# Decoding float64 weights with two rectifiers and an AND in place of three activations, with four of the five hand-written orders dealt anew

## The chip, the cores and the metric

The kernel runs on one core of a Trainium2 chip. Its engines are TensorE (PE, with its weight loads shown apart as PEld), VectorE (DVE), ScalarE (ACT), GpSimd (POOL) and SyncE (SP, which here only issues DMAs). The metric is device time in microseconds (us), the median of several runs. Before the change it is 758.82 us, the median of 3 runs from 758.43 to 759.01.

## The reference

Attention between tokens and a small recurrent state, in both directions, followed by a gated feed-forward layer:

```python
B, H, S, Ns, D = (8, 8, 512, 32, 64)
scores = scale * np.matmul(x, state.transpose(0, 1, 3, 2))
a = softmax(scores);  xread = np.matmul(a, state)
scores2 = scale * np.matmul(state, x.transpose(0, 1, 3, 2))
a2 = softmax(scores2); sread = np.matmul(a2, x)
x = concatenate([xread, sread])      # as (B*S', H*D) rows, S' = 512 + 32
rms = np.sqrt(np.mean(x * x, axis=-1, keepdims=True) + 1e-06)
xn = x / rms * rms_g
silu = g * (1.0 / (1.0 + np.exp(-g)))          # g = xn @ w_gate
return (silu * (xn @ w_val) @ w_out).astype(np.float32)
```

There are 4352 rows of 512, and 1536 hidden columns. The three weight matrices arrive as float64 values, two 32-bit words to each number, while the rest is float32. [...]

## The kernel before, in words

**Weights.** The three matrices are read as 18 pieces of 1 MB ("raw", four buffers; piece 0 in two halves). Each piece holds 128x1024 numbers. `exponents()` (lines 231 to 248) works on ScalarE: it takes the top 16 bits of each number (sign, eleven bits of exponent, four of mantissa) and, in three activations, L240, L243 and L246, turns them into the 16 bits of a bfloat16 that is a signed power of two. Prelu is a rectifier with another slope on its negative side, and `FLAT` sets the ratio of the two slopes. `values()` (lines 250 to 282) works on VectorE: L267 masks the top mantissa bits and puts the leading one in, L270 adds the low word to 2^32 times that, and L276 multiplies the mantissa by the power of two from ScalarE and writes the float32 weight. Every third piece ends with a write of the finished weights to DRAM (L280), from which later batches fetch them (`fetch`, L189). Conversion tiles (`conv`) have two buffers each.

**Batches.** Eight batches of 512 tokens follow each other. For batch b the kernel computes the reading of the state (`tokens_read`: scores L361, maximum, EXP, sums, transposes, the squares of what is read, their sum, a power on POOL at L293, its turning back along rows on PE at L300, and the scaling at L501). For batches after the first the sum of the squares goes through `rms_on_blocks`: a block sum on PE (L415), `ss` on VectorE (L420), `mean_root` on POOL (L293), `along_rows` on PE (L300). `states_read` is the other direction; L557 and L572 are its products. Because the state has 32 rows and the weights are reused, the weights are first multiplied by the batch's state (`own_weights`, products L616, copies L628 on ScalarE, sums L643 to L646 on POOL), and tokens then multiply by these.

Batch 0 runs plain: `hidden` (products L659 for gate and value, silu L665, gated product L669 on VectorE, PSUM pool `vps` of two banks) and `project_as_ready` (L866). Later batches use schemes with seven products: `hidden_seven` (products L763, copies L810, L813 and L815 out of PSUM on ScalarE, silu L817, sums L826 and L839 on VectorE) and `project_twice` (products L1066, copies L1076 into tiles "kept", combination L1092 to L1097 on POOL, and `stores()` by L1174). The hidden layer of a batch runs in six groups. The tiles "g" of `hidden_seven` and the tiles "kept" of blocks p1, u2 and c21 share the two buffers of tag "g". The block c21 is the last of a batch, so its buffer is the one that group 1 of the next batch writes next (L810).

**Order.** Each engine runs its instructions in the order in which they are issued, SyncE too, and the kernel issues them in an order written out by hand. Every stretch of work is a Python generator, called by a letter, and a string of letters says which generator takes its next step. In ORDER (batch 0 and all conversion) "e" is one step of `exponents`, "d" one of `values`, "z" a filler product on PE (`keep_awake`, L1198), "a" and "s" the readings for batch 0, "A" and "S" those for batch 1, "v" `own_weights`, "h", "t", "u" products, silu and gated product of the hidden layer, "p" and "c" projection, "w" the first steps of batch 1 and "k" sums of weights. FIRST is the string of batch 1, PERIOD that of batches 2 to 6, LAST that of batch 7, and STATES that of the state rows. In these "h", "t", "u" are products, copies and sums of `hidden_seven`, "p", "c", "k", "o" are products, copies, sums and stores of `project_twice`, "v" and "x" products and copies of `own_weights`, "w" the first products of the next batch, "a" and "s" the readings for the next batch, "f" a fetch of weights (L189), "g" a fetch of a weight quarter (L1012), and "l" the loads of state and x (L129, L134). Letters of different engines set no order between those engines; waits for data and for free buffers do that.

Of the kernel before, what the change touches and what calls it, by code (L numbers as in the profile page):

```python
# [8 lines left out]
F32 = mybir.dt.float32  # L9
I32 = mybir.dt.int32  # L10
U32 = mybir.dt.uint32
U16 = mybir.dt.uint16
I16 = mybir.dt.int16
BF16 = mybir.dt.bfloat16
ALU = mybir.AluOpType
ACTF = mybir.ActivationFunctionType
# [3 lines left out]
P = 128  # L20
RAW_AHEAD = 4
W_BUFS = 3
FLAT = 1793.0

ORDER = (
    "ddzzzzzzzzzezzzeezaaaaaaaaaaaaddaezddaseaaazzaeaaazzdaaaazdeezzzazzaaaazeeaaaadd"
    "aaadaaeAdadsdeezezAdavaaAvAAAAvhehteeAeAdddduhhppdAddtdeeedvvvudeeedphhdtheeddtA"
    "ddddeupdAAAdhAdedeeuedppvpsdAvvddAedhhpetudeeeddhtsAAdhudpAeppdddeAAeedddvAdsvvA"
    "eedphhtuseessseedddeeAhtsdhesppsdvdupdvvdhheeAddAdAtsshtpAudApAedpdhededdveuAApA"
    "AAvvheAdAtSAASSeSSdphSddShAtASuShAkuSSwwpwwkcpSScpSkkckpkcwkkkkkwwwwk"  # L30
)

PERIOD = (
    "vlhhatthhtaxxhvuxuthhthuhtauuhhtuhuhuthtahtuaaahuhhtuhuhuxhxtutxhthukkkhtaakavfx"
    "xxvgahuhuthuuuxhthhuuxtahtaaaaahuaxhuthhtuhhthhthhsppusuuuuffutaauuhpsspuppppukp"
    "ukkkkckkaakkgppkkcpppakooskakakakkppppacpppappppcckpfppcakakapppaakkkasskkgkaagg"
    "pppppppppppaakakkooakgapssskaaakkkoosspppcfpaawwsslpssxxxpcoowxxxfg"
)

FIRST = (  # L40
# [4 lines left out]
    "xssswxlscxxcoxofxg"  # L45
)
LAST = (
    "vxhhffththhtuhhhavuttuuhhtfuhhgxxthhhuuuxxtuthuhtthuhuxhutuvxxxvhthhutkxghhtuhut"
    "kxxhuukhtuhthhthhhhhuuuuttuthhhuuuuhtuhuutuupphuukkppcpapkkkkkpppppppppppkkkpcpp"
    "ckkppkckpkkpkpckkkpppkkkpkoppkpppagcpppppfkpkkkkkkkkppaaaapkpggppppacpcggooooooo"  # L50
    "a"
)
STATES = (
    "hththtyyhuhuhhttuhhhyyytyuhutuhhhutthtuyyhhuuyhhthhhuyututyyyhhtyuhhthuuuhhuhtth"
    "ythuuuyyyutuhuhuytuuyhthhuuhthtuhuhutuuppkhpuucppkkccpkpkpc"
)


# [1 line left out]
def kernel(  # L60
# [21 lines left out]
    VE, SE, GE, TE = nc.vector, nc.scalar, nc.gpsimd, nc.tensor  # L82
# [13 lines left out]
    consts = ctx.enter_context(tc.tile_pool(name="consts", bufs=1))  # L96
# [34 lines left out]
    def load_x(b, *queues):  # L131
# [6 lines left out]
        for c in range(NC):  # L138
# [10 lines left out]

    GE.tensor_tensor(out=consts.tile([P, NC], F32, name="first_pow"), in1=mhalf,  # L150
                     in0=ones.to_broadcast([P, NC]), op=ALU.pow)
    bounds = consts.tile([P, 3], F32, name="bounds")
    for i, bound in enumerate((-896.0 - 7.5 / 16, 1.0, 255.0 * 128)):
        GE.memset(bounds[:, i:i + 1], bound)
    rms_g = consts.tile([P, NI], F32, name="rms_g")

# [22 lines left out]
    raw = {}  # L179
# [11 lines left out]
    def home(k):  # L191

        mp, kind = divmod(k, 3)
        if kind == 2:
            return wo[:, 2 * mp:2 * mp + 2].rearrange("p m (i f) -> p m i f", f=P)
        return (w_sb[mp] if kind else new_w(mp))[:, :, :, kind, :]
# [12 lines left out]
    def load_piece(k):  # L209
        for _ in load_parts(k):  # L210
            pass

    def parts(k):

        n = pieces[k].shape[1]
        return (slice(0, n // 2), slice(n // 2, n)) if k == 0 else (slice(0, n),)
# [3 lines left out]
    exs = {}  # L220

    def columns(k, a):
        n = pieces[k].shape[1]
        return slice(8 * P * a.start // n, 8 * P * a.stop // n)

    def exponents():

        for k in range(len(pieces)):  # L230
            for a in parts(k):
                if k not in raw:
                    yield from range(3)
                    continue
                if a.start == 0:
                    exs[k] = conv.tile([P, 8 * P], I16, name="ex")
                    lin = conv.tile([P, 8 * P], F32, name="lin")
                ex, line = exs[k][:, columns(k, a)], lin[:, columns(k, a)]
                half = raw[k][:, columns(k, a)].bitcast(I16)[:, :, 3::4]
                SE.activation(out=line, in_=half, func=ACTF.Prelu, scale=1.0 / 16,  # L240
                              bias=bounds[:, 0:1], alpha=1.0 / FLAT)
                yield
                SE.activation(out=ex, in_=line, func=ACTF.Prelu, bias=bounds[:, 1:2],  # L243
                              alpha=FLAT)
                yield
                SE.activation(out=ex.bitcast(U16), in_=ex, func=ACTF.Relu, scale=128.0,  # L246
                              bias=bounds[:, 2:3])
                yield

    def values():  # L250
        for k in range(len(pieces)):
            for a in parts(k):
                if a.start == 0:
                    to = home(k)
                    if k in raw:
                        top_ = conv.tile([P, 8 * P], I32, name="top")
                dst = to[:, a]
                if k not in raw:
                    src = pieces[k].rearrange("p a (c f) -> p a c f", f=P)
                    for i in range(a.start, a.stop):  # L260
                        nc.sync.dma_start(out=to[:, i], in_=src[:, i])
                    yield from range(3)
                else:
                    top, r = (t[:, columns(k, a)] for t in (top_, raw[k]))
                    hi = r[:, :, 1]
                    man = r.bitcast(F32)[:, :, 0]
                    VE.tensor_scalar(top, hi, 0xfffff, 0x100000,  # L267
                                     op0=ALU.bitwise_and, op1=ALU.bitwise_or)
                    yield
                    VE.scalar_tensor_tensor(out=man, in0=top, scalar=2.0 ** 32,  # L270
                                            in1=r.bitcast(U32)[:, :, 0], op0=ALU.mult, op1=ALU.add)
                    yield
                    yield
                    man, ex = (t.rearrange("p (a c f) -> p a c f", f=P, c=dst.shape[2])
                               for t in (man, exs[k][:, columns(k, a)].bitcast(BF16)))
                    VE.scalar_tensor_tensor(out=dst, in0=man, scalar=-2.0 ** -52, in1=ex,  # L276
                                            op0=ALU.mult, op1=ALU.mult)
                if a.stop == pieces[k].shape[1]:
                    if k % 3 == 1:
                        nc.sync.dma_start(out=w_d[k // 3], in_=w_sb[k // 3])  # L280
                    raw.pop(k, None)
                    load_piece(k + RAW_AHEAD)
                yield
# [887 lines left out]
    def store_tokens(b):  # L1171
        def store(r, c0, n, ot):
            rows_ = out[T * b:T * b + S, c0:c0 + n]
            nc.sync.dma_start(out=rows_[P * r:P * r + P], in_=ot)  # L1174
        return store
# [48 lines left out]
    for k in range(2, RAW_AHEAD):  # L1224
        load_piece(k)
    load_state(1)
    load_x(1)
    streams = {"a": tokens_read(0), "s": states_read(0), "A": tokens_read(1), "S": states_read(1),
               "e": exponents(), "d": values(),
               "v": (step for mp in range(NM // 2) for part in own_weights(0, mp) for step in part),  # L1230
               "h": of_batch_0(0), "t": of_batch_0(1), "u": of_batch_0(2),
# [5 lines left out]
    with tc.manual_schedule(**by_hand):  # L1237
# [7 lines left out]
        for b in range(1, B):  # L1245
            h, t, u = hidden_seven(S, weights_of(b), lambda b=b: tokens_of(b), True)
            p, c, k, o = project_twice(b, store_tokens(b))
# [19 lines left out]
        p, c, k = project_seven(NT, store_states, nc.scalar)  # L1267
# [34 lines left out]
```

## Time and profile before

| | |
|---|---|
| time, median of 3 | 758.82 us |
| span of the profiled execution | 756.2 us |
| PE busy in 0 to 32.5 us | 27.64 us |
| PE busy in 32.5 to 133 us | 100.45 us |
| PE busy in 133 to 213 us (batch 1) | 76.44 us |
| PE busy in 293 to 373 us | 80.00 us |
| PE busy in 614 to 756 us | 138.31 us |
| granted TensorE clock, every window | 1.00 |

The profiled execution spans 756.2 us from the first to the last instruction; against the median some 2.6 us lie around it. Batch 1 starts at 133 us, and a batch in PERIOD takes about 80 us. In the lines of the profile the letter L with a number is the line of the kernel; a group has its count after x, then the busy time in us, the mean duration in ns, and the idle time of the engine ahead of it with what ended it. In the timeline the first number is the start in us, the second the duration. A "DMA issues" line ends with the median time from issue to landing.

### The profile page before, as it was taken

What the parts mean: (1) busy time and instruction counts of PE and PEld (TensorE: products, weight loads), DVE (VectorE), ACT (ScalarE), POOL (GpSimd) and SP (SyncE); (2) the same over time, 40 slices, a digit from 0 to 9 for tenths busy, and PEclk for the clock granted to TensorE, in tenths of its full rate; (3) what the DMA queues carried; (4) which work ended last, traced back from release to release, by engine and by line L of the source; (5) the groups of instructions that cost most, each with busy time, mean ns of one, the idle gap of its engine ahead of it and who ended that gap; (6) DMA issues with size and microseconds to landing.
All of it is one profiled execution on the core that took longest, in us unless ns stands there. A gap on an engine that the chain in (4) does not pass through costs nothing.

```text
span 756.2 us, 14360 instructions
## 1 busy us (share of the span) xinstructions
PE 743.2 (98%) x5618; PEld 592.0 (78%) x5618; DVE 578.7 (77%) x979; ACT 351.7 (47%) x546; POOL 294.2 (39%) x380
## 2 busy tenths in 40 slices
PE   8999999999899999999999999999999999999998
PEld 6534444778768898879877997799788987899997
DVE  3887776679957996689947994799579965787961
ACT  5998965553235523643255425543456236411220
POOL 2000003892584326532474129312842275323600
PEclk9999999999999999999999999999999999999999
DMA  9986954695576176725684377517661865132311
GB/s 281 281 299 227 314 211 151 248 294 163 201 228 240 32 291 209 281 56 198 243 284 112 135 274 253 175 69 299 215 225 27 305 204 218 51 98 114 140 56 29
DMA packets 61891, 146.17 MB, mean 193 GB/s; under 512 B 15744, under 2 KB 32640, under 8 KB 54912
## 3 DMA queue, kind: packets, MB, share of 16 engines
q1 hardware_dynamic: 48704, 125.78, 47.8%
q10 hardware_dynamic: 13120, 19.47, 8.9%
q8 instruction: 45, 0.74, 0.4%
q14 instruction: 22, 0.18, 0.1%
HBM read 116.46 MB, written 28.77 MB: 192 GB/s over the span
## 4 chain that ended last, share of the span: by engine, by line
PE 91%; DVE 5%; ACT 3%; issue 1%; POOL 0%; DVEq 0%; POOLq 0%
PE f L763 38%; PE f L1066 28%; PE pv L659 5%; PE f L866 5%; PE at L616 3%; PE pv L616 3%; PE f L929 2%; PE f L1198 2%; PE at L557 1%; PE at L361 1%; PE at L487 1%; DVE hb L1125 0%; PE at L300 0%; ACT ex L243 0%; PE at L334 0%
## 5 line engine op out<-in xcount | busy, mean ns | idle before, releaser
L763 PE MATMUL f<-aT_s,v 128*128 128x256 f32 x504 | 119.6, 382 | 0.0
L763 PEld LDWEIGHTS f<-aT_s,v 128*128 128x128 f32 x504 | 94.5, 190 | 24.8 <-issue 8.4
L1092 POOL TENSOR_TENSOR kept<-kept 128x256 f32<-128x256 f32 x28 | 23.1, 824 | 174.9 <-DVE kept L1106 173.8
L826 DVE TENSOR_TENSOR g<-g,f 128x512 f32<-128x512 f32 x84 | 57.4, 686 | 40.0 <-PE f L763 35.9
L1076 ACT COPY kept<-f 128x512 f32<-128x512 f32 (+1 forms) x56 | 29.6, 532 | 123.9 <-PE f L1066 82.2
L763 PE MATMUL f<-aT_t,vs 128*128 128x256 f32 x336 | 87.1, 383 | 0.0
L1066 PE MATMUL f<-w,h 128*128 128x128 f32 x588 | 74.6, 276 | 0.9 <-DVE h L1116 0.8
L763 PEld LDWEIGHTS f<-aT_t,vs 128*128 128x128 f32 x336 | 62.5, 190 | 15.4 <-POOL vs L643 4.2
L1066 PEld LDWEIGHTS f<-w,h 128*128 128x128 f32 x588 | 69.6, 192 | 5.3 <-issue 4.1
L817 ACT ACTIVATE hb<-g 128x1024 f32<-128x1024 f32 x42 | 44.4, 1058 | 56.9 <-DVE g L826 56.8
L643 POOL TENSOR_TENSOR vs<-v 128x256 f32<-128x256 f32 x42 | 31.4, 748 | 79.5 <-ACT v L628 79.5
L293 POOL TENSOR_TENSOR ri<-ss,mhalf 128x4 f32<-128x4 f32 x8 | 10.7, 1341 | 116.7 <-DMA w_m<-w_d 84.1
L815 ACT COPY g<-f 128x512 f32<-128x512 f32 x42 | 24.6, 586 | 45.0 <-PE f L763 45.0
L763 PE MATMUL f<-aT_t,v 128*128 128x256 f32 x168 | 43.5, 381 | 1.6 <-DVE c L826 1.6
L866 PE MATMUL f<-wo,hb 128*128 128x512 f32 x96 | 44.8, 603 | 0.0
L659 PE MATMUL pv<-aT_s,v 128*128 128x512 f32 x96 | 43.9, 595 | 0.0
L763 PE MATMUL f<-aT_s,vs 128*128 128x256 f32 x168 | 43.6, 382 | 0.0
L839 DVE TENSOR_TENSOR hb<-hb,c 128x512 f32<-128x512 f32 (+1 forms) x48 | 36.6, 763 | 7.9 <-ACT hb L817 7.2
L839 DVE TENSOR_TENSOR hb<-hb,f 128x512 f32<-128x512 f32 (+1 forms) x48 | 31.0, 646 | 15.1 <-PE f L763 15.1
L1066 PE MATMUL f<-wo,h 128*128 128x128 f32 x336 | 42.2, 275 | 0.0
L1066 PE MATMUL f<-wo,hb 128*128 128x128 f32 x336 | 42.1, 275 | 0.0
L826 DVE TENSOR_TENSOR c<-c,f 128x512 f32<-128x512 f32 (+1 forms) x48 | 31.2, 651 | 12.6 <-PE f L763 12.6
(204 smaller groups left out, 1657.7 us busy)
## 6 DMA issues: line engine op xcount, KB each, us to landing
w_m<-w_d SPq DMA_DIRECT2D x48, 1024.0 KB, 5.8
w<-t_d SPq DMA_DIRECT2D x49, 576.0 KB, 5.1
out_dram<-kept SPq DMA_DIRECT2D x56, 128.0 KB, 1.9
raw<-in_moe_w_val_dram SPq DMA_DIRECT2D x6, 1024.0 KB, 5.4
raw<-in_moe_w_out_dram SPq DMA_DIRECT2D x6, 1024.0 KB, 8.5
w_d<-w_m SPq DMA_DIRECT2D x6, 1024.0 KB, 4.9
x_b<-in_x_dram SPq DMA_DIRECT2D x6, 1024.0 KB, 7.7
x_d<-xB ACTq DMA_DIRECT2D x6, 1024.0 KB, 4.2
```

Of the source, the lines that this page charges most:

```text
L616: TE.matmul(out=pv[e][Ns * j:Ns * j + Ns, :], lhsT=stT_g[b][D * e:D * e + D, j, :], rhs=w[D * e:D * e + D, j].rearrange("p m k f -> p (m k ...
L643: GE.tensor_tensor(out=vs[:, 0], in0=a21, in1=a22, op=ALU.add)
L659: TE.matmul(out=to[0], lhsT=lhs(i, k), rhs=r, start=(i == 0), stop=(i == len(rhs) - 1))
L763: TE.matmul(out=ps[:, i, 0:half], lhsT=l[:, i, :], rhs=r, start=(start and i == 0 and k == 0), stop=(k == len(lhs) - 1), skip_group_check= ...
L815: SE.copy(gates(q)[1], q["x"][:, :, 0:half])
L817: SE.activation(out=hb[:, 2 * mp:2 * mp + 2, 0:n].rearrange("p m (c t) -> p m c t", c=2), in_=q["g"][:, :, :, 0:half], func=ACTF.Silu if s ...
L826: VE.tensor_tensor(out=to, in0=to, in1=q[ps][:, :, 0:half], op=ALU.add)
L839: VE.tensor_tensor(out=part, in0=part, in1=val, op=ALU.mult)
L866: TE.matmul(out=banks[r], lhsT=hb[:, m, P * r:P * r + P], rhs=wo[:, m, :], start=(m == 0), stop=(m == NM - 1))
L1066: TE.matmul(out=to[half][:, slot, :], lhsT=lhs[:, k, :], rhs=rhs[:, k, :], start=(fresh and n in (0, 4) and k == 0), stop=(k == QM - 1), s ...
L1076: SE.copy(k[:, 4 * i:4 * i + 4 - i], banks[name][i])
L1092: GE.tensor_tensor(out=k[:, 1:3], in0=k[:, 0:1].to_broadcast([P, 2, QD]), in1=k[:, 1:3], op=ALU.add)
```

## The change

`exponents()` uses two activations instead of three. The first now reads the top 16 bits as unsigned and with a negative scale, the second brings the result straight into the 16 bits of a bfloat16, in a form that has bits too many; `values()` then clears these with one bitwise AND on VectorE, in place, on the two-byte numbers taken as 512 32-bit words in each partition (256 for the halves of piece 0), between L270's and L276's places. The constants follow (`FLAT`, and two columns of `bounds` instead of three). The letter "e" has two steps per piece in place of three: 38 in place of 57 in ORDER. ORDER, PERIOD, LAST and STATES are dealt anew; FIRST is not touched. PERIOD, LAST and STATES hold the same letters as before in another order.

```diff
-FLAT = 1793.0
+FLAT = 128.0 * 1792.0
...
 ORDER = (
-    "ddzzzzzzzzzezzzeezaaaaaaaaaaaaddaezddaseaaazzaeaaazzdaaaazdeezzzazzaaaazeeaaaadd"
-    "aaadaaeAdadsdeezezAdavaaAvAAAAvhehteeAeAdddduhhppdAddtdeeedvvvudeeedphhdtheeddtA"
-    "ddddeupdAAAdhAdedeeuedppvpsdAvvddAedhhpetudeeeddhtsAAdhudpAeppdddeAAeedddvAdsvvA"
-    "eedphhtuseessseedddeeAhtsdhesppsdvdupdvvdhheeAddAdAtsshtpAudApAedpdhededdveuAApA"
-    "AAvvheAdAtSAASSeSSdphSddShAtASuShAkuSSwwpwwkcpSScpSkkckpkcwkkkkkwwwwk"
+    "eezzzzdzdzzzzzdaazadaaaaaaaaazezdadeazadadaazaeaazzzaaazzezaazzzaazazaaazadaadee"
+    "aadaaAdaedasseAAAvvvaAAasAdAdhhAhtsddeudpdsdddedtAepdhudvvdevphdesephtddAshededd"
+    "uAhAApAddtddvSpdedusAvvhethdhphdeAddedteAddSesueASddupAppddedAdvevddveAdAphthdSd"
+    "AsseedSpudAsddApepvedhvSdtAvhAhuSdehApdAtAdepAehASAuddddedAtSdAhdpvpvAvdhhduAete"
+    "uSphAdtAhpAdkusAppccApSwkskwSSkwkpkSkwwcwkwkwckkkw"
 )
 
 PERIOD = (
-    "vlhhatthhtaxxhvuxuthhthuhtauuhhtuhuhuthtahtuaaahuhhtuhuhuxhxtutxhthukkkhtaakavfx"
-    "xxvgahuhuthuuuxhthhuuxtahtaaaaahuaxhuthhtuhhthhthhsppusuuuuffutaauuhpsspuppppukp"
-    "ukkkkckkaakkgppkkcpppakooskakakakkppppacpppappppcckpfppcakakapppaakkkasskkgkaagg"
-    "pppppppppppaakakkooakgapssskaaakkkoosspppcfpaawwsslpssxxxpcoowxxxfg"
+    "vaxhahththtfhuhuhhutaahtaxhttauhhuaxvuuhxhhttuhgtuhhxhxtuhuuhtauhhaututkkvvhtxah"
+    "xxuhuhhhautxhtahxkuuuktaahautashhuuuthstuxhhfguhtutuhahuutahuususpaphlpukfpakppk"
+    "pcpckppkpupaafkpkkkkppkkapgppcppakkkkkkppppappsacpappacakpakkgasppkapksppakpkpck"
+    "pooaapkpakapogaksappkapakakaagposkpkspssaawsosowsglppfwcxxsxcfxoxox"
 )
...
-    bounds = consts.tile([P, 3], F32, name="bounds")
-    for i, bound in enumerate((-896.0 - 7.5 / 16, 1.0, 255.0 * 128)):
+    bounds = consts.tile([P, 2], F32, name="bounds")
+    for i, bound in enumerate((1152.0 - 1.0 / 32, -FLAT)):
...
                 if k not in raw:
-                    yield from range(3)
+                    yield from range(2)
...
-                half = raw[k][:, columns(k, a)].bitcast(I16)[:, :, 3::4]
-                SE.activation(out=line, in_=half, func=ACTF.Prelu, scale=1.0 / 16,
+                half = raw[k][:, columns(k, a)].bitcast(U16)[:, :, 3::4]
+                SE.activation(out=line, in_=half, func=ACTF.Prelu, scale=-1.0 / 16,
                               bias=bounds[:, 0:1], alpha=1.0 / FLAT)
                 yield
-                SE.activation(out=ex, in_=line, func=ACTF.Prelu, bias=bounds[:, 1:2],
-                              alpha=FLAT)
-                yield
-                SE.activation(out=ex.bitcast(U16), in_=ex, func=ACTF.Relu, scale=128.0,
-                              bias=bounds[:, 2:3])
+                SE.activation(out=ex, in_=line, func=ACTF.Prelu, scale=-128.0 * FLAT,
+                              bias=bounds[:, 1:2], alpha=1.0 / FLAT)
                 yield
...
                     yield
+                    bits = exs[k][:, columns(k, a)].bitcast(I32)
+                    VE.tensor_scalar(bits, bits, -0x7f0080, None, op0=ALU.bitwise_and)
                     yield
```

LAST and STATES are left out of the diff: their letters are as many of each as before, in another order. The AND takes the step that was empty in `values()` before, so the letter "d" keeps its number of steps.

## The prediction

> **What bounds the kernel now.** I read the page from its head down: the busy shares, the chain that ended last, then the groups of the first stretch, and after them the timeline and the DMA issues around one boundary between two batches.
>
> ```profile
> PE 743.2 (98%) x5618; PEld 592.0 (78%) x5618; DVE 578.7 (77%) x979; ACT 351.7 (47%) x546; POOL 294.2 (39%) x380
> PE 91%; DVE 5%; ACT 3%; issue 1%; POOL 0%; DVEq 0%; POOLq 0%
> ```
>
> TensorE is busy for 98% of the span and carries 91% of the chain. A saving on ScalarE or VectorE is worth something only where TensorE waits, and a new order of the work is worth what it adds to or takes from those waits. A table of windows shows where they are: PE is busy 80.00 of 80 us from 293 to 373 and again from 373 to 453, 100.45 of 100.5 from 32.5 to 133, and only 27.64 of the first 32.5. So the first 32.5 us can give something; the batches of PERIOD can only lose.
>
> ```profile
> L240 ACT ACTIVATE lin<-raw,bounds 128x1024 f32<-128x1024 int16 x17 | 21.2, 1249 | 0.0
> L270 DVE SCALAR_TENSOR_TENSOR raw<-top,raw 128x1024 f32<-128x1024 int32 x17 | 20.9, 1226 | 0.3
> L243 ACT ACTIVATE ex<-lin,bounds 128x1024 int16<-128x1024 f32 x17 | 19.6, 1153 | 0.4
> L246 ACT ACTIVATE ex<-ex,bounds 128x1024 uint16<-128x1024 int16 x17 | 19.5, 1148 | 0.3
> L267 DVE TENSOR_SCALAR top<-raw 128x512 int32<-128x512 int32 x2 | 1.0, 522 | 5.1 <-DMA raw<-in_moe_w_gate_dram 5.1
> ```
>
> These are the groups of the conversion, forms kept apart. The third activation, L246, goes.
>
> **The sum is made against** the profiled execution: span 756.2 us plus 2.6 us around it, 758.8, which is the median.
>
> **Part 1, the conversion.** ScalarE loses 17 x 1.148 + 2 x 0.726 = 21.0 us. VectorE gains 19 ANDs, 17 of 128x512 int32. No row shows an AND alone; L267, two bit operations on the same shape, took 522 ns on average, and 687 at twice the width. I take 0.52 (bounds 0.43, the faster of the two, and 0.69), so about 9.4 us of VectorE. None of it counts as such: from 32.5 to 133 VectorE is busy 74.6 and ScalarE 81.4 of 100.5 us, and PE covers both. If that cover goes, an AND costs its 0.52 in each chain it stands in. The other constants cost nothing: same two operations, same shapes.
>
> **Part 2, the start (new ORDER).** PE's first 32.5 us are one chain: the state and x turned, scores, exponentials, squares, the root mean square, and the first hidden product, L659, at 32.46.
>
> ```profile
> 9.33 0.27 PE L311 MATMUL at<-ident,rows 128*128 128x128 f32 x1
> 28.50 1.40 POOL L293 TENSOR_TENSOR ri<-ss,mhalf 128x4 f32<-128x4 f32 x1 [22.67 <-DVE ss L397]
> 32.46 1.88 PE L659 MATMUL pv<-aT_s,v 128*128 128x512 f32 x4
> ```
>
> Before L311 stand 13 of the idle fillers (z, L1198). The new order has 10; the early ones take 427 ns a record, so L311 moves from 9.33 to about 8.05 (the state rows landed at 8.04), 1.3 us. Further on, the turned x waits for one activation less on ScalarE, and the conversion's last product L276 (1.22 us, at 27.03) no longer stands between the second square (26.43) and ss (28.26). Followed by hand through the new letters: scores 13.36 becomes 12.3, the maximum 15.87 becomes 15.0, ss 28.26 becomes 26.9, the pow 28.50 becomes 27.1, L659 about 30.4. A gain of 2.05 (1.5 to 2.5). The raw pieces are issued in the same order, so no new wait on DMA.
>
> Against it stands one new wait. Hidden group 5's value product needs the PSUM bank (two in the pool) that group 4's gated product, L669, must first read. On VectorE that L669 now stands behind the AND and last product of piece 9, the top bits of piece 10 and a maximum; and on ScalarE piece 9's two activations stand behind group 4's silu. Chain: 0.60 + 1.25 + 1.15 + 0.52 + 1.21 + 0.6 + 0.6 + 0.69 = 6.6. PE's work beside it: two hidden halves of four 512-column products (0.43 each, 1.72 a half) and one pair of projections, 5.25. Stall 1.4 (0 to 2, with the AND at 0.43 and other queues late, or at 0.69 and the weights of group 1 late by 0.45). First stretch: -2.05 + 1.4 = **-0.65** (-2.5 to +0.5).
>
> **Part 3, PERIOD: the root mean square.** Batches 2 to 6 run PERIOD. After the block sums L415, ss and the pow run on VectorE and POOL, then PE turns the result, L300; between them stand four steps of six products (L1066). The new order has three.
>
> ```profile
> 371.96 0.29 PE L415 MATMUL at<-part,groups 128*128 128x16 f32 x2
> 373.04 1.39 POOL L293 TENSOR_TENSOR ri<-ss,mhalf 128x4 f32<-128x4 f32 x1 [1.54 <-DVE ss L420]
> 374.86 0.60 PE L300 MATMUL at<-ident,ri 128*128 128x128 f32 x4
> ```
>
> In batch 1, where three steps already stand there, L415 is at 212.11, the pow at 213.26 for 1.39 and L300 at 214.70, with 0.38 us that no product fills. 5 x 0.38 = **+1.9** (0 to 2.5).
>
> **Part 4, PERIOD: SyncE's queue at the end of a batch.** Here lies most of my forecast. The kept block c21 uses one of the two buffers of tag "g". Next batch, the first copy of group 1 (L810) takes the same buffer, and must wait until both c21 stores have landed. The queue now, and that copy:
>
> ```profile
> 377.20 1.17 SPq L1174 DMA_DIRECT2D out_dram<-kept  x2
> 378.47 0.37 SPq L189 DMA_DIRECT2D w_m<-w_d  x1
> 378.93 0.40 SPq L134 DMA_DIRECT2D x_b<-in_x_dram  x1
> 385.80 1.67 SPq L1174 DMA_DIRECT2D out_dram<-kept  x2
> 387.56 0.38 SPq L189 DMA_DIRECT2D w_m<-w_d  x1
> 387.99 0.44 SPq L1012 DMA_DIRECT2D w<-t_d  x1
> 388.48 2.06 SPq L129 DMA_DIRECT2D rows<-in_state_dram  x4
> ```
>
> ```profile
> 388.94 0.58 ACT L810 COPY g<-f 128x512 f32<-128x512 f32 x1 [0.94 <-DMA out_dram<-kept]
> ```
>
> Already the copy waits 0.94 for the stores (two of 128 KB, 2.6 us to landing). They go out on a queue that has just emptied: x, issued at 378.93, took 7.8 and landed at 386.7. In the new order the last stretch reads: stores of u2, fetch of a weight quarter, load of x, two weight fetches, and only then the two c21 stores. How long a small transfer takes behind large ones, the issues from 387.5 to 391 and one at 211 show:
>
> ```profile
> w<-t_d SPq DMA_DIRECT2D x1, 576.0 KB, 6.5
> rows<-in_state_dram SPq DMA_DIRECT2D x4, 16.0 KB, 5.7
> ```
>
> ```profile
> out_dram<-kept SPq DMA_DIRECT2D x2, 128.0 KB, 5.1
> ```
>
> The 16 KB rows, issued at 388.48, land at about 394.7, just behind the quarter (387.99 + 6.5 = 394.5); the 128 KB stores at 211 take 5.1, not 2.6, behind a quarter. Landings follow the order of issue. [...]
>
> Time from the pow's end (374.43 in the shown batch). u2's stores at +2.8 as now; the quarter at +4.05, landing 4.0 later as one alone does (4.1 at 372): +8.05. Then x: now it lands 3.2 after the weights ahead of it (378.47 + 5.0 = 383.5), so 3.1 more: +11.15. The weight fetches: the one at 390.64 took 6.8, to 397.4, 2.9 behind the quarter; two are +16.95. The c21 stores cannot be issued before +11.4, as now (385.80): POOL makes their block after the sums that follow the pow, in the order it has now. By then x has landed and both weight fetches stand ahead of them, so they land 0.7 behind the second: +17.65. On PE, after the pow: L300, L557, two sets of weights, L572, two steps, another set and L311 make 6.3 to the first product of the next batch, and group 1's second product, which needs that copy, stands nine products of 0.87 on, as the weights that stood between (1.0) are moved behind it: +14.3. It needs landing + 0.1 + 0.58 (copy) + 0.08: +18.4. Stall 4.1 (bounds 3.0 and 5.5 with weight fetches of 2.5 or 3.6 behind others, as at 124 to 134). Behind the waiting copy on ScalarE stand the rest of group 1's copies and the copies of the next weights; PE waits for all of them through this one place. It happens where x is loaded, after batches 2, 3, 4 and 5: 4 x 4.1 = **+16.4**. After batch 6 no x is loaded: +0.6 (0 to 2). After batch 1 the unchanged FIRST string comes first and only the earlier place of the product counts: +0.7 (0.3 to 1).
>
> **Part 5, LAST and STATES** hold the same letters in another order. I found no wait longer than those now: 0 (-0.5 to +0.5).
>
> **Sum:** -0.65 + 1.9 + 16.4 + 0.6 + 0.7 = +19.0; 758.8 + 19.0 = **777.8**. Own range of this case: +11.9 to +27, 770.7 to 786.
>
> **The rivals.** (1) *Stores overtake.* The c21 stores share the engines with the weight fetches and land 3.0 after their issue at +11.4, as now (388.84 by the copy that follows): +14.4, and +15.2 with the copy against the product's +14.3, 0.9 each: -0.65 + 1.9 + 4 x 0.9 + 0.6 + 0.7 = +6.1: 764.9. Against it: the rows of 16 KB and the stores at 211. (2) *Faster: the landing is early.* If the c21 stores land like those at 377, 2.1 after issue, that is +13.5, the copy ends before PE comes to +14.3, and every term of Part 4 is nothing. Then the start decides: with its 2.05 and the waits at group 5 and at L300 at their lower bounds, as PE's stream comes to them a little later than reckoned, 756.8. It decides from a landing under +13.6; for it speaks only that row, whose queue held nothing large. (3) *The long pauses slow PE.* At the start, records of L1198 are 427 ns apart and later 216, so PE runs at half pace after idling. If each 4 us pause is followed by some 3.4 us at half pace, each boundary costs 1.7 more: 777.8 + 6.8 = 784.6. Against it: pauses up to 1.85 us in batch 1 leave the granted clock at 1.00. [...] (4) *The conversion changes nothing else:* an AND at 0.69 only adds 0.2 to the stall at group 5; inside every range.
>
> **How the numbers follow.** My forecast 0.63, the slowed clock 0.09, overtaking stores 0.13, faster 0.10, and 0.05 for an early landing with the start's gain and the other waits in balance (758 to 760). A change under 0.2% (1.5 us) cannot be told from none. Slower: 0.63 + 0.09 + 0.13 = 0.85; same 0.05; faster 0.10. The range 762 to 786 leaves out the last two, and little at the top: under 2 in 10.
>
> **What the changed profile would show.** No L246 group of three activations; an AND group near 0.5 us x17; L659 near 30.4; one pause near 1.4 us before group 5's value product; L300 some 0.4 late in each PERIOD; and in batches 3 to 6 the second L810 copy released by a store that took 6 us where it now takes 2.6, PE idle about 4 us there. I am wrong if those stores land in 3 us, or if that copy is done before PE needs it.

## The result and the profile after

The changed kernel takes 800.07 us (median of 4 runs, 799.2 to 801.3) against 758.72 before (median of 4 taken with them): 1.0549 times as long, 95% interval 1.0534 to 1.0564. The direction was right and the size was not: 777.8 was forecast, with 762 to 786 as the range.

The page of the changed kernel, from its head (busy times and the chain that ended last). The lines of the changed kernel are one to three lower than before from L244 on; L762 is the old L763, L809 the old L810, L414 the old L415, L299 the old L300, L496 the old L497.

```profile
PE 759.8 (95%) x5618; PEld 597.6 (75%) x5618; DVE 602.4 (76%) x998; ACT 331.9 (42%) x529; POOL 295.0 (37%) x379
PE 58%; DVE 26%; POOL 6%; DMA 4%; issue 3%; ACT 2%; SPq 0%; DVEq 0%; ACTq 0%; POOLq 0%
```

PE carried 91% of the chain and now carries 58%; VectorE has 26%, POOL 6% and the DMAs 4%. ScalarE lost 19.8 us of work and VectorE gained 23.7 us of busy time, of which 7.8 are the 19 ANDs (7.2 for the 17 full ones, 0.423 each). The rest, 15.9 us, is work that was there before and takes longer.

Where the 41.3 us between the two profiled executions (797.5 and 756.2 us) lie follows from the starts of the pow on POOL, one in each batch; the first and the last of those that bound PERIOD, in the changed kernel and then in the one before:

```profile
212.85 1.39 POOL L292 TENSOR_TENSOR ri<-ss,mhalf 128x4 f32<-128x4 f32 x1 [2.15 <-DVE ss L419]
654.67 1.02 POOL L292 TENSOR_TENSOR ri<-ss,mhalf 128x4 f32<-128x4 f32 x1 [3.95 <-DVE ss L419]
```

```profile
213.26 1.39 POOL L293 TENSOR_TENSOR ri<-ss,mhalf 128x4 f32<-128x4 f32 x1 [2.16 <-DVE ss L420]
613.62 1.39 POOL L293 TENSOR_TENSOR ri<-ss,mhalf 128x4 f32<-128x4 f32 x1 [1.55 <-DVE ss L420]
```

Batch 1's products begin at 131.32 instead of 133.08: 1.76 gained. The pow at the end of batch 1 starts at 212.85 instead of 213.26: 0.41 of that is left. The five batches of PERIOD, from there to the last such pow, take 441.82 us instead of 400.36: 41.46 lost. Behind it come 142.8 instead of 142.6: 0.2 lost. So -0.41 + 41.46 + 0.2 makes the 41.3, and all of it is PERIOD. Its five batches cost 5.0, 7.3, 8.5, 10.7 and 10.0 us more than the same batches before.

One boundary between two batches in the changed kernel: SyncE's queue, then ScalarE, then PE (start, duration, engine, line, and the idle time ahead of it with what ended it).

```profile
388.71 0.81 SPq L1173 DMA_DIRECT2D out_dram<-kept  x2
389.63 0.39 SPq L1011 DMA_DIRECT2D w<-t_d  x1
390.11 0.40 SPq L134 DMA_DIRECT2D x_b<-in_x_dram  x1
390.60 1.28 SPq L189 DMA_DIRECT2D w_m<-w_d  x2
397.29 0.81 SPq L1173 DMA_DIRECT2D out_dram<-kept  x2
```

```profile
402.58 0.59 ACT L809 COPY g<-f 128x512 f32<-128x512 f32 x1 [3.81 <-DMA out_dram<-kept]
```

```profile
399.37 1.03 PE L762 MATMUL f<-aT_t,v 128*128 128x256 f32 x4
403.31 2.01 PE L762 MATMUL f<-aT_t,vs 128*128 128x256 f32 x4 [2.91 <-ACT g L809]
405.11 1.85 PE L762 MATMUL f<-aT_s,vs 128*128 128x256 f32 x4
406.80 1.03 PE L762 MATMUL f<-aT_s,v 128*128 128x256 f32 x4
```

This is the boundary as forecast: the quarter, x and two weight fetches stand ahead of the c21 stores; the stores go out at 397.29, 11.3 us after the pow's end; group 1's copy waits for them until 402.58, and PE's next product until 403.31. At the four boundaries where x is loaded PE loses 3.4, 3.1, 4.2 and 4.6 us in this way, counted from the start of one product to the start of the next, less the usual 0.22; the idle time alone, the figure in brackets, is 0.16 less each time. The second thing to see is the length of the records behind the pause: four took 1.03 us as usual at 406.80, 2.01 and 1.85 right behind the pause. A table of windows shows the clock granted there (columns: PE, its weight loads, VectorE, ScalarE and POOL busy, then the granted clock, the DMA share and GB/s):

```profile
399.40:403.30 3.90, 1.00 (x5) 0.56 (x4) 2.71 (x5) 0.72 (x2) 0.74 (x2) 1.00 1.04 420
403.30:406.80 3.50, 3.49 (x9) 2.77 (x10) 0.00 (x0) 1.43 (x3) 2.81 (x4) 0.51 0.39 150
```

The end of a batch shows what the prediction did not have. PE waits for VectorE's block sums ahead of L414, 1.29 us of idle time there:

```profile
380.68 1.50 PE L1065 MATMUL f<-wt,hb 128*128 128x128 f32 x12
383.48 0.37 PE L414 MATMUL at<-part,groups 128*128 128x16 f32 x2 [1.29 <-DVE part L411]
```

```profile
377.55 2.11 DVE L496 TENSOR_TENSOR sq<-sq 128x512 f32<-128x512 f32 x2
379.58 0.81 DVE L1113 TENSOR_TENSOR h<-hb 128x384 f32<-128x384 f32 x1
380.31 1.21 DVE L496 TENSOR_TENSOR sq<-sq 128x512 f32<-128x512 f32 x1
382.65 0.69 DVE L411 TENSOR_REDUCE part<-sq 128x16 f32<-128x512 f32 x1
```

The three additions of squares take 0.97, 1.21 and 1.21 us. The same three took 0.68 each before (L497; count, then the shortest, median and longest in ns):

```profile
L497 DVE TENSOR_TENSOR sq<-sq x21: 682/684/694, 109.0 to 608.3; 128x512 f32<-128x512 f32 x21
```

While they run, POOL combines block p5:

```profile
377.25 0.73 POOL L1091 TENSOR_TENSOR kept<-kept 128x256 f32<-128x256 f32 x1 [11.89 <-DVE kept L1105]
378.06 1.06 POOL L1093 TENSOR_TENSOR kept<-kept 128x256 f32<-128x256 f32 x1
```

In the old order the second half of p5 came behind the second of these additions, and POOL worked mostly beside transposes and sums that follow. The third addition did run beside POOL's first operation there, but it had begun 0.16 us earlier (367.75 and 367.91): it took its 0.68, and POOL's operation 1.11 where 0.73 is usual. The new order has p5 ahead of all three.

### The profile page after: what moved, and what is told of

Read it like the earlier page. It is cut to its first block, busy times and chain, and to the rows that moved or that the text cites. A ratio compares the mean times of both kernels' runs of the same rounds, so it can differ in the third digit from the quotient of the medians.

```text
span 797.5 us, 14345 instructions
## 1 busy us (share of the span) xinstructions
PE 759.8 (95%) x5618; PEld 597.6 (75%) x5618; DVE 602.4 (76%) x998; ACT 331.9 (42%) x529; POOL 295.0 (37%) x379
## 4 chain that ended last, share of the span: by engine, by line
PE 58%; DVE 26%; POOL 6%; DMA 4%; issue 3%; ACT 2%; SPq 0%; DVEq 0%; ACTq 0%; POOLq 0%
PE f L762 25%; PE f L1065 11%; PE f L865 5%; PE pv L658 5%; DMA out_dram<-kept 3%; PE at L615 3%; PE f L928 2%; DVE kept L1105 2%; DVE sq L496 2%; DVE hb L838 2%; DVE h L1113 2%; DVE h L1119 2%; DVE hb L1124 2%; PE f L1197 2%; DVE h L1115 1%
## 5 line engine op out<-in xcount | busy, mean ns | idle before, releaser
L762 PE MATMUL f<-aT_s,v 128*128 128x256 f32 x504 | 121.4, 384 | 2.3 <-ACT g L814 2.3
L762 PEld LDWEIGHTS f<-aT_s,v 128*128 128x128 f32 x504 | 95.2, 192 | 25.2 <-issue 6.8
L762 PE MATMUL f<-aT_t,vs 128*128 128x256 f32 x336 | 91.2, 396 | 15.9 <-ACT g L809 15.9
L762 PEld LDWEIGHTS f<-aT_t,vs 128*128 128x128 f32 x336 | 62.6, 194 | 39.2 <-issue 21.9
L1091 POOL TENSOR_TENSOR kept<-kept 128x256 f32<-128x256 f32 x28 | 21.1, 754 | 180.3 <-DVE kept L1105 177.9
L762 PE MATMUL f<-aT_s,vs 128*128 128x256 f32 x168 | 45.8, 397 | 0.0
L762 PE MATMUL f<-aT_t,v 128*128 128x256 f32 x168 | 43.8, 383 | 1.8 <-DVE c L825 1.6
L627 ACT COPY v<-at 128x512 f32<-128x512 f32 x52 | 29.4, 587 | 31.5 <-PE at L615 31.5
```

What stands on the lines that cost most here:

```text
L627: SE.copy(v[:, e].rearrange("p m k f -> p (m k f)"), pv[e])
L762: TE.matmul(out=ps[:, i, 0:half], lhsT=l[:, i, :], rhs=r, start=(start and i == 0 and k == 0), stop=(k == len(lhs) - 1), skip_group_check= ...
L1091: GE.tensor_tensor(out=k[:, 1:3], in0=k[:, 0:1].to_broadcast([P, 2, QD]), in1=k[:, 1:3], op=ALU.add)
```

## The experiments

**The queue.** Only the last two weight fetches move behind the c21 stores.

```diff
-"...ppfwcxxsxcfxoxox"
+"...ppwcxxsxcxoxoxff"
```

> The changed kernel, with only the two weight fetches at the end of PERIOD moved behind the two c21 stores in SyncE's order. Theory A (the stores are held behind the loads ahead of them, and group 1's first copy waits for them): the quarter and x have landed by +11.2 us after the pow, the stores go out at +11.3 and land by +14, the copy no longer holds PE; the waits of 3.1 to 4.6 us at four boundaries (15.3 us in all) fall under 0.5 each, and with them the slow clock behind them (about 6 us): 800 - 21 = 779 (777 to 782). Theory B (the copy waits for POOL's late block, not for the queue): the stores still go out at +11.3, and the time stays at 799 to 801.

Measured: 781.74 us (780.93 to 785.0), 18.3 less than the changed kernel. The boundary now, SyncE, ScalarE and PE:

```profile
386.17 0.40 SPq L134 DMA_DIRECT2D x_b<-in_x_dram  x1
393.21 0.81 SPq L1173 DMA_DIRECT2D out_dram<-kept  x2
394.12 1.37 SPq L189 DMA_DIRECT2D w_m<-w_d  x3
```

```profile
395.52 0.58 ACT L809 COPY g<-f 128x512 f32<-128x512 f32 x1 [0.83 <-PE f L762]
```

```profile
396.25 1.10 PE L762 MATMUL f<-aT_t,vs 128*128 128x256 f32 x4
```

The copy waits for PE's own product and no longer for a store, and PE has no pause. Theory B falls: POOL's block is as late as ever. The gain is 3 us under the 21 expected. The moved fetches have a price: 0.3 us of a new wait at this boundary, for the weights that are now fetched later (L615 at 399.50), and more behind batch 6:

```profile
652.79 1.09 PE L615 MATMUL at<-w_m,stT_g 64*32 64x512 f32 x16 [1.94 <-DMA w_m<-w_d]
```

**The clock.** Filler products, 3.0 us of them, fill PE's pause at the same place.

```diff
...
+                if mp == 1 and 3 <= b <= 6:
+                    ps = aps.tile([P, 2, P], F32, name="at")
+                    for _ in range(7):
+                        TE.matmul(out=ps, lhsT=ident, rhs=ident.unsqueeze(1).to_broadcast([P, 2, P]),
+                                  start=True, stop=True)
                 product(q["x"], q["s"][1], tt[1], False)
...
```

> The changed kernel with seven filler products (3.0 us) on PE ahead of the second product of group 1 in batches 3 to 6, where PE waits 3.1 to 4.6 us. Theory A (PE's clock falls because it idles there): the granted clock stays at 1.00 behind the pauses, the 1.7, 3.1 and 1.7 us at half pace go, the waits themselves stay hidden under the fillers: 800 - 6.4 = 793.7. Theory B (the slow records behind the pauses have another cause, or the fillers only add to the path): 800 to 812.

Measured: 793.44 us (792.89 to 794.23), 6.6 less, though PE has more to do. The rows of the fillers and of what follows, and the window behind the pause:

```profile
400.26 3.19 PE L791 MATMUL at<-ident 128*128 128x256 f32 x14
404.95 1.10 PE L762 MATMUL f<-aT_t,vs 128*128 128x256 f32 x4 [1.50 <-ACT g L814]
```

```profile
404.00:408.00 4.00, 3.05 (x20) 2.29 (x28) 0.76 (x2) 2.15 (x4) 2.55 (x4) 1.00 0.30 118
```

Over the four boundaries the copy comes as late as before, 17.1 to 18.2 us after the pow's end against 16.6 to 18.2 (at the one shown it is 1.6 later). Here 1.5 us of pause remain, but the records behind it are back at 1.1 us and the clock at 1.00. So at the boundaries it is PE's idling that slows the clock, and this costs some 6.6 us in the changed kernel. It is the third rival, which was given 6.8 us and a chance of 0.09.

**POOL beside VectorE.** POOL's four additions for p5 are left out in batches 2 to 6.

```diff
+            if what != "p5" or not 2 <= b <= 6:
                 GE.tensor_tensor(out=k[:, 1:3], in0=k[:, 0:1].to_broadcast([P, 2, QD]), in1=k[:, 1:3],
...
```

> The changed kernel without POOL's four additions that combine block p5 in batches 2 to 6 (this part of the computation is left out); VectorE's instructions and their order stay. Theory A (VectorE's additions of the squares, L496, run at 1.05 us instead of 0.64 because POOL works at the same time, and so the block sums reach PE 1.3 to 1.5 us late in each of five batches): L496 back to 0.64, PE's wait before L414 under 0.3, 800 - 6.5 = 793.5. Theory B (VectorE has too much ahead of the block sums, whatever POOL does): L496 unchanged, the wait stays at 1.3, 800.

Measured: 794.62 us (790.29 to 796.35), 5.5 less. L496 by its line, first in the changed kernel and then in this one (count; shortest, median and longest in ns):

```profile
L496 DVE TENSOR_TENSOR sq<-sq x21: 683/975/1211, 102.4 to 650.1; 128x512 f32<-128x512 f32 x21
```

```profile
L496 DVE TENSOR_TENSOR sq<-sq x21: 682/684/689, 102.2 to 644.8; 128x512 f32<-128x512 f32 x21
```

```profile
383.08 0.29 PE L414 MATMUL at<-part,groups 128*128 128x16 f32 x2
```

VectorE's order is the same, each addition is back at 0.684, and PE does not wait before L414. The slowdown is POOL's doing. The 5.5 us are not the price of the wait, though: in this kernel new waits of 0.6 to 2.3 us stand ahead of L556 at six boundaries, and the pauses for the stores are others (1.8 to 3.9 us of idle time in place of 2.9 to 4.4). In the changed kernel an addition that began while POOL was at work took 0.29 to 0.53 us longer (969 to 1211 ns, 15 of them, where the other six took 683 or 684).

**VectorE's lateness by itself.** On top of the first experiment, two of the three additions of squares are left out for batches 3 to 7.

```diff
+                if b < 3 or i + j == 1:
                     VE.tensor_tensor(out=sq[:, i, :], in0=sq[:, i, :], in1=sq[:, j, :], op=ALU.add)
```

> The kernel of the first experiment (late fetches, 781.7) without two of the three additions of squares on VectorE for batches 3 to 7 (that part of the sum of squares is left out), 1.9 us less work for VectorE right ahead of the block sums in each PERIOD batch. Theory A (VectorE is late at the end of a batch, and PE's 1.47 us before L414 is all of that): the wait goes, 781.7 - 5 x 1.5 = 774.2 (773 to 775.5). Theory B (as in the repaired PERIOD, what is won there comes back at the next place within the same batch): 778 or more.

Measured: 774.43 us (773.09 to 775.9), 7.3 less than the first experiment, and PE runs into L414 without a pause:

```profile
374.40 1.50 PE L1066 MATMUL f<-wt,hb 128*128 128x128 f32 x12
375.74 0.29 PE L414 MATMUL at<-part,groups 128*128 128x16 f32 x2
```

The wait before L414 is thus worth some 7.3 us of the loss (five times 1.46), and inside the five batches no other wait takes its place when VectorE has less to do: they take 414.3 us where the first experiment has 422.7. Part of that is lost again behind batch 6, in the wait for the late weights (2.5 us in this profile, whose mean granted clock is 0.996).

**The rest of PERIOD.** Five small moves, the fetches of the first experiment among them.

```diff
# four places of the string PERIOD
-"taahautas" ... "kpakkgas" ... "kpakapogaksappkapaka" ... "pssaawsosowsglppfwcxxsxcfxoxox"
+"tahtaauas" ... "kpkakgas" ... "kpaaaakpogksppkapaka" ... "psspaawsosowsglpwcxxsxcxoxoxff"
```

> The changed kernel with five small moves in PERIOD: the two last weight fetches behind the c21 stores (as in the first experiment, 781.7), the three additions of squares ahead of the second addition to p5, group 4's third copy ahead of the copy of the scores, one inner sum ahead of a product of the exponentials, and the turning back of the root one step of six products later. Theory A (PE's waits of 1.47, 0.73, 0.53 and 0.24 us in each of five batches come from these places): 781.7 - 5 x 2.7 = 768. Theory B (the new order has less slack everywhere, so a wait taken away comes back at the next place): over 776.

Measured: 780.85 us (778.51 to 781.47), within a microsecond of the first experiment, so theory A fails. Theory B fits: the five batches take 421.6 us for 422.7. One end of a batch there:

```profile
461.97 0.37 PE L414 MATMUL at<-part,groups 128*128 128x16 f32 x2 [0.87 <-DVE part L411]
```

```profile
456.00 2.55 DVE L496 TENSOR_TENSOR sq<-sq 128x512 f32<-128x512 f32 x3
459.52 0.97 DVE L1115 TENSOR_TENSOR h<-h,hb 128x384 f32<-128x384 f32 x1
```

Of the three additions only the second is still slow (0.68, 1.22 and 0.69), as POOL's first operation for p5 still falls beside it, and L1115 takes 0.97 where 0.55 is usual. PE's wait before L414 is 0.87 instead of 1.29. The wait of 0.53 us at an inner sum went away, but the product of the exponentials that had to make room now keeps PE some 0.6 at L486, which reads it. From 456 to 462 VectorE is busy 5.90 of 6 us: with no idle time left there, a move on VectorE's queue mostly chooses who waits.

**PERIOD alone, and all but PERIOD.** Two kernels split the change.

```diff
# the changed kernel, PERIOD as before
-    "vaxhahththtfhuhuhhutaahtaxhttauhhuaxvuuhxhhttuhgtuhhxhxtuhuuhtauhhaututkkvvhtxah"
+    "vlhhatthhtaxxhvuxuthhthuhtauuhhtuhuhuthtahtuaaahuhhtuhuhuxhxtutxhthukkkhtaakavfx"
...
# the kernel before, PERIOD as changed
-    "vlhhatthhtaxxhvuxuthhthuhtauuhhtuhuhuthtahtuaaahuhhtuhuhuxhxtutxhthukkkhtaakavfx"
+    "vaxhahththtfhuhuhhutaahtaxhttauhhuaxvuuhxhhttuhgtuhhxhxtuhuuhtauhhaututkkvvhtxah"
...
```

> The changed kernel with PERIOD as it was before; conversion, ORDER, LAST and STATES as changed. Theory A (all of the loss is PERIOD's order): batch 1's pow came 0.4 us earlier than before and the stretch behind the last PERIOD took 0.25 longer, so 758.7 - 0.2 = 758.5 (757.5 to 759.5). Theory B (the conversion or the shifted start feeds the loss through the transfers): more than 765.

> The kernel before, with only PERIOD as changed (three activations, the old ORDER, LAST and STATES). Theory A (PERIOD's order alone makes the loss): the five PERIOD batches cost 41 us more than before, 758.7 + 41 = 800 (796 to 803). Theory B (the new PERIOD is bad only together with the new start or the new conversion): under 785.

Measured: with the old PERIOD 758.01 us (ratio to before 0.9990, interval 0.9978 to 1.0001), and with the new PERIOD alone 803.12 (802.9 to 803.34). The second is at the upper end of what theory A gave (796 to 803). The conversion has no part in the loss. The full change is some 3 us faster than the new PERIOD alone; how much of this is the conversion and the start, and how much another length of the pauses and of the slow clock, was not taken apart.

**Held stores in the old order.** The kernel before, with its two c21 stores last.

```diff
-"...pcoowxxxfg"
+"...pcwxxxfgoo"
```

> The kernel before, with one move in PERIOD: the two c21 stores behind the last weight fetch and the last quarter in SyncE's order. Theory A (held stores alone make the wait): after the pow x lands at +12.3, the fetch and the quarter that now go ahead at about +15 and +17, the stores at +17.8; the copy is done 0.76 later, PE's second product of group 1 stands at +15.8: 2.7 us of wait at each of four boundaries, 758.7 + 11 = 770 (766 to 772), the clock at 1.00 since the pauses are short. Theory B (such a store is only late together with the rest of the new order): 758 to 760.

Measured: 777.83 us (775.88 to 779.35), 19 more than before and 8 more than expected. The waits are as expected, 2.1 to 3.2 us at each of four boundaries. What was not expected is the clock. It falls behind the pause, here in two windows, the pause and what follows, and the mean of 0.991 over the 775.0 us of the profile is worth 14 us at half pace, four times the 3.41 us of one slow stretch in the changed kernel:

```profile
309.80:312.00 2.20, 0.23 (x2) 0.06 (x1) 0.69 (x1) 0.76 (x2) 1.62 (x3) 1.00 1.02 294
312.00:316.00 4.00, 4.00 (x11) 3.19 (x12) 0.24 (x1) 0.90 (x2) 0.00 (x0) 0.57 0.31 129
```

So one wait on one queue, moved into an order that had none, gives nearly half of the change's loss by itself, and some 1.7 us behind each pause, from the half pace (0.57 over 4 us), are part of that.

**What the conversion and the new start are worth.** PERIOD, LAST and STATES as before; and then, in ORDER, the last output block's copy and store ahead of the second set of batch 1's weights.

```diff
 # second kernel, end of ORDER
-"...cwkwkwckkkw"
+"...ccwkwkwkkkw"
```

> The changed kernel with PERIOD, LAST and STATES as before: conversion and ORDER alone. Theory A (the start gives 1.8 to 2.3 us, batch 1's wait for an output store takes 0.6 to 1.0 of it back, the tail is as before): 758.7 - 1.2 = 757.5. Theory B (whatever the start gains is lost again in batch 1): 758.7 within 0.5.

> As the kernel with conversion and ORDER alone, and in ORDER the last output block's copy and store go ahead of the second set of batch 1's weights and the weight fetch that it issues. Theory A (batch 1's second L810 copy waits for that store, which lands behind the fetch): the store lands at about 137 instead of 139.8, PE's wait of 0.6 to 1.0 us at 139 goes, 0.6 to 1.0 us less than the other. Theory B (the wait moves to the fetch, which is now later): no difference.

Measured: 757.69 us for the first (ratio 0.9978, interval 0.9962 to 0.9994) and 755.96 for the second (0.9955, 0.9942 to 0.9968). Batch 1's second copy, in the first kernel and in the second:

```profile
138.01 0.59 ACT L809 COPY g<-f 128x512 f32<-128x512 f32 x1 [1.71 <-DMA out_dram<-ot]
```

```profile
137.51 0.57 ACT L809 COPY g<-f 128x512 f32<-128x512 f32 x1
```

It is the same mechanism in small: a store behind a weight fetch, a copy that needs the store's buffer. With the store first the copy no longer waits, nor does PE, which waited 0.91 us for it. The two kernels are 1.7 us apart where 0.6 to 1.0 was expected; the mean granted clock of their runs was 0.9973 and 0.9988, which is worth up to 1.1 us of the 757, and why the clock differs is open. The second kernel is faster than both kernels of the case, 0.45% under the one before.

## Why the prediction was right or wrong

- **The conversion** was right. ScalarE lost 19.8 us for the 21.0 forecast. The AND took 423 ns (L271, 17 of them), at the lower bound of 0.43 rather than at the 0.52 taken. It is hidden, as said: PE is busy in 102.00 of the 102 us from 30 to 132.
- **The start** was right in kind and wrong in size. L310 moved from 9.33 to 8.80, the pow from 28.50 to 26.96 (27.1 forecast) and the first hidden product from 32.46 to 31.13, 1.3 us instead of 2.05. Behind the pow something stands that no term had: the clock is at 0.50 from 27.88 to 31.29, though PE had no pause (busy 3.38 of the 3.41 us ahead of that).

```profile
28.36:31.13 2.77, 2.77 (x20) 2.62 (x13) 1.96 (x6) 1.89 (x4) 0.00 (x0) 0.50 0.94 259
```

  In the kernel before, the clock is at 1.00 through all of the start. Why it falls here is open; the fewer fillers are a candidate that no run tested.
- **The stall at group 5** was wrong: it is not there. Group 5's value product started at 67.10, right behind a projection, while the gated product L668 of group 4 only ran from 67.92 to 68.60. The chain had been timed well, with its end forecast 6.6 us behind the gate's product at 61.95 and found at 68.60. But the product did not wait for that: its weight load at 66.68 carries a wait on the semaphore that ScalarE's silu counts up, and group 5's own silu ran from 65.59 to 66.19. So the bank that I took to be group 4's must be another one; which one is open.
- **Batch 1** takes back 1.35 us of the 1.76 gained; the sum had nothing there. 1.0 of it is PE's wait for the second L809 copy, which waits for the output store behind the weight fetch. That 0.41 is left, near the 0.65 of the forecast, is luck: a stall that did not come, a slow clock and this loss make up for each other.
- **The boundaries** were right in mechanism and size. The stores went out at +11.3 (forecast +11.4) and landed at +16.5 to +18.1 (forecast +17.65), the copy that waits for them started just behind, PE's product stood at +14.3 as forecast, and PE lost 15.3 us in all where 16.4 were forecast. The small terms came out smaller: from the last pow of PERIOD to the end 0.2 is lost (0.6 after batch 6), and after batch 1 PE waits no longer than 0.2 for that copy (0.7).
- **The clock** is one of two steps that failed. It stood as a rival at 0.09, against it the short pauses of batch 1. The fillers show 6.6 us. The 3.4 us at half pace that it put behind each pause stood on no row of before; the changed kernel shows 3.41 us behind two of its four pauses for the stores, 6.82 behind another and none behind the first. The pauses of 1.0 to 1.85 us did leave the clock at 1.00 in both kernels of the case, but there was no row for a pause between 2 and 5 us, and it should have been a bound of the sum, not a rival. Short pauses are no safe ground either: in the old order with its stores last an idle time of 1.97 us, up to 311.98, was followed by a clock of 0.57 over 4 us.
- **The root mean square in PERIOD** is the step that failed most. "Between them stand four steps of six products. The new order has three" looked at the stretch behind L414 and found 1.9 us. There 0.24 us a batch is lost (twelve products at 384.44 took 1.56 for 1.32), 1.2 in all. The larger wait stands ahead of L414, where VectorE was not followed: 1.29 us of idle time a batch, 1.46 from one product's start to the next, 7.3 us in all by the experiment. No term of the sum was a wait for VectorE in PERIOD. There are more of them: 0.46 us before a product that needs ScalarE's copy L814, which stands behind a copy of the scores that waits for VectorE (0.73 with the pipeline refilled), 0.35 before an inner sum's product (0.53):

```profile
342.23 1.99 PE L762 MATMUL f<-aT_s,v 128*128 128x256 f32 x8 [0.46 <-ACT g L814]
371.75 0.94 PE L1065 MATMUL f<-w,h 128*128 128x128 f32 x6 [0.35 <-DVE h L1115]
```

- **The sum**: -0.4 to the end of batch 1, 15.3 waiting for the stores, 6.6 of slow clock, 7.3 before L414 make 28.8 of the 41.3. Of the other 12 or so, 1.2 are L299's and 6.3 the two waits just named (5 x 1.26), and 0.2 lies behind PERIOD. Some 4 to 5 us are small waits that no run took apart, and the five moves show that taking such a wait away need not shorten the batch. The range could not have held the result: even the upper bounds of all terms together give +28.5, and +35.3 with the slow clock, as no bound allowed for VectorE.

## What to carry to other kernels

In a queue that runs in order, a store that must land before a buffer is used again belongs ahead of the loads that nobody waits for yet (18.3 us here); look for the wait at the next user of the buffer, not at the store. A pause of a few microseconds on PE can cost more than its length (2.91 us here, and 3.41 us at a clock of 0.50 behind them), and cheap filler products in it can pay (6.6 us). When an order is dealt anew, follow each engine's queue up to every place where the bound engine waits for it, with the durations that its operations have beside the work they will now run beside.

## What the runs showed of the hardware

- The additions of squares on VectorE slowed down beside POOL's additions: 684 ns alone, 969 to 1211 where POOL was at work when they began, and 684 in the old order where the addition began 0.16 us ahead of POOL's operation, which took 1.11 us for 0.73.
- The granted clock fell to 0.50 for 3.41 us, or twice that, behind idle times of 2.91, 4.06 and 4.43 us in the changed kernel, and not behind every pause. One of 3.28 us was followed by a clock of 1.00 there:

```profile
316.19 1.10 PE L762 MATMUL f<-aT_t,vs 128*128 128x256 f32 x4 [3.28 <-ACT g L809]
```

```profile
311.19:314.60 3.41, 1.71 (x8) 1.16 (x7) 3.41 (x6) 0.08 (x1) 1.46 (x3) 1.00 1.00 403
314.60:318.01 3.41, 1.82 (x8) 1.48 (x9) 0.01 (x1) 2.15 (x4) 1.33 (x2) 1.00 0.68 284
```

  Where the pause fell mattered as much as its length. The slow stretches of the changed kernel begin and end whole multiples of 3.41 us apart (403.35 to 406.76, 492.10 to 498.92 and 584.25 to 587.66), so a grid can be laid over its trace. The stretch of this grid ahead of each of these three had PE busy 0.50, 0.41 and 0.00 us of 3.41. The pause above fell across two, with 1.71 and 1.82 busy, while the idle time of 1.97 us at 310 in the old order with its stores last left PE busy 1.44 of the 3.41 us ahead of a slow stretch. In the changed kernel, from 35 us on, those three stretches and the first half of the slow one at 492.10, with 2.34 busy, were followed by a slow one, and none of the 217 others, with 1.72 or more. In the kernel before, with the clock at 1.00 from 35 us to PE's last product, no 3.41 us between have PE busy less than 1.77. The slow clock at the start of the changed kernel, behind a busy PE (3.38 of 3.41 us), does not fit this.
- Stores of 128 KB landed in the order of issue behind 1 MB fetches each time: the c21 stores of the changed kernel took 4.8 to 6.4 us to landing at the four boundaries, where 1.8 to 2.7 was usual before. At none of them did a store overtake a fetch.
